# A recurrence in 64 by 64 quarters: products, masks and loads from step 2 on, in a kernel of recurrence and two gated layers on one core

## The chip, the core and the metric

The kernel runs on one core of a Trainium2 chip. The core has TensorE (PE; PEld is its weight load), VectorE (DVE), ScalarE (ACT), GpSimd (POOL) and SyncE (SP), whose instruction stream issues nearly all DMAs here. The metric is the device time of one execution in microseconds (us). Before the change three runs took 878.15, 882.37 and 885.78 us, so the median is 882.37 us.

## What is computed

The reference is a linear recurrence over 768 positions for 4 batches of 8 heads of 48 features, and then two gated layers on its output (3072 rows of 384 features):

```python
for t in range(S):                       # S = 768, state: [4, 8, 48, 48]
    cur = einsum('bhd,bhe->bhde', u * kt, vt)
    y[:, :, t] = einsum('bhd,bhde->bhe', rt, state + cur)
    state = w[:, :, None] * state + einsum('bhd,bhe->bhde', kt, vt)
x = y as [3072, 384]
x = (x @ w_a * (x @ w_b)) @ w_out                    # 384 -> 1536 -> 384
x = ((x @ w1 * (x @ w2)) @ w3) @ w_out2              # 384 -> 1024 -> 384
```

## The kernel before

**The recurrence in chunks.** The 768 positions are cut into six steps of C = 128, and a step has four units, one for each batch; unit `u = 4 * step + batch`, 24 in all. A unit multiplies r and k by tables of powers of w, forms for each head the 128 by 128 scores k·r of positions inside the chunk, masks them to earlier positions, puts the u-weighted value on the diagonal, and adds (scores × v) to (state × r). It then decays the state and adds k × v.

**Heads on the array.** Heads lie in four pairs (`NP = 4`): the even head of a pair at partitions 0 to 47, the odd one at 64 to 111 (`XR`). So the scores' products (`scores_f`, line 343) use 48 rows and all 128 columns, two at a time in the two row halves, each row half with a PSUM bank of its own. `y_mm` multiplies the block-diagonal state by r for a whole pair (line 414, 112 by 112), then all 128 positions of v by the masked scores (line 425, 128 rows by 48 columns, two at a time in the two column halves). `s_mm` (line 497) is 128 rows by 48 columns as well. In steps 0 and 1, where the weights have to be read and converted at the same time, `scores_h` and `scores_d` (lines 358 to 373) already cut a chunk's positions into halves of 64: their products use 48 rows by 64 columns, and four stand in the array at a time.

**Masks and copies.** `a_evac` (line 397, DVE) masks the scores of four heads at a time out of PSUM, `a_diag` (line 403, DVE) writes the diagonal. The output of `y_mm` is split into a rounded high part (`y_evac_h`, ACT) and a low part (`y_evac_l`, DVE); the features of heads 6 and 7 are moved to their places by small DMAs (`y_shuffle`). `s_decay` is ACT, `s_upd` DVE.

**Loads.** A unit loads r and k transposed (`load_rk`, one DMA) and r, k, v in natural order (`load_nat`, one DMA of 576 KB from step 2 on), both on SP's queue, into two buffers each. On the natural copy POOL forms r·u·k (`prep_d`), which DVE sums to the diagonal (line 329), and POOL scales k (`k_nat`).

**The gated layers.** For each step, `block1` goes through twelve slices of 128 hidden features: 18 products of 128 by 128 by 512 (`ab_mm`, line 557) into two of the three banks `ab0` to `ab2`, ACT and DVE form the gated value and its high and low part, and 9 products (`m_mm`, lines 574 to 576) add it to three banks `m0` to `m2`. The second layer (from about 440 us) needs no recurrence.

**What sets the order.** All work is recorded as tasks with an engine, an assumed duration, dependencies, a priority and buffers (`Task`, `Buf`, `Slot`). `plan` (line 95) then walks through an assumed time and writes the instructions of every engine in the order in which they would start; the engines run that order, and wait for each other by semaphores. From step 2 on the recurrence's PSUM tiles come from the two banks `at0` and `at1` alone (`at_c = at_s`), in steps 0 and 1 from these and the `ab` banks.

The functions that the change touches, and what calls them:

Of the kernel before, what the change touches and what calls it, by code (L numbers as in the profile page):

```python
# [7 lines left out]
F32 = mybir.dt.float32  # L8
# [11 lines left out]
NP = H // 2  # L20
# [11 lines left out]
HALF = C // 2  # L32

# [131 lines left out]
def rwkv_moe_kernel(ctx, tc, rkT, nat, wu, wab, wout, w12, w3T, wo2, r_in, k_in, v_in, w_in, u_in, out):  # L165
# [13 lines left out]
    with tc.manual_schedule():  # L179
# [21 lines left out]

        XR = [(0, D), (64, 64 + D)]


# [126 lines left out]
        def k_nat(u):  # L331
            if u < NU - B:
# [3 lines left out]
                eng.tensor_tensor(out=kn_t[u], in0=k, in1=tnat.rearrange("p a x d -> p (a x d)"), op=ALU.mult)  # L336

        def scores_f(ps, r, k):

            for p in range(NP):  # L340
                s = slice(p * C, (p + 1) * C)
                for x, (r0, r1) in enumerate(XR):
                    mm(ps[x][:, p, :], lhsT=k[r0:r1, s], rhs=r[r0:r1, s], start=True, stop=True)  # L343

        def scores(u):
            for x in range(2):
                at_ps[u, x] = at_tile([128, NP, C])
            scores_f([at_ps[u, x] for x in range(2)], flat(rf_t[u]), kf_t.pop(u))
# [45 lines left out]
        def a_evac(u, hf):  # L394
            if hf == 0:
                a_t[u] = att.tile([128, H, C], F32, name="a_sc", bufs=1)
            nc.vector.tensor_tensor(
                out=a_t[u][:, 4 * hf:4 * hf + 4, :], in0=at_ps.pop((u, hf)),
                in1=mask.rearrange("p (o n) -> p o n", o=1).to_broadcast([128, 4, C]), op=ALU.mult)

        def a_diag(u, hf):
            d = d_t[u].rearrange("p (q x) -> p x q", x=2)[:, hf, :]
            nc.vector.copy_predicated(
                out=a_t[u][:, 4 * hf:4 * hf + 4, :],
                mask=ident.bitcast(I32).rearrange("p (o n) -> p o n", o=1).to_broadcast([128, 4, C]),
                data=d.rearrange("p (h o) -> p h o", o=1).to_broadcast([128, 4, C]))

        def y_mm(u):
            c, b = divmod(u, B)
# [6 lines left out]
            if c == 1:  # L416
                for n, e in enumerate((HALF, 128)):
                    for h in range(H):
                        r0, r1 = XR[h % 2]
                        mm(ps[r0:r1, h // 2, n * HALF:(n + 1) * HALF], lhsT=v[0:e, h * D:(h + 1) * D],  # L420
                           rhs=a[0:e, n, h % 2 * 4 + h // 2, :], start=False, stop=True, skip_group_check=True)
            else:
                for h in range(H):
                    r0, r1 = XR[h % 2]
                    mm(ps[r0:r1, h // 2, :], lhsT=v[:, h * D:(h + 1) * D], rhs=a[:, h % 2 * 4 + h // 2, :],  # L425
                       start=False, stop=True, skip_group_check=True)
            rf_t.pop(u)

        def y_0(u):
# [5 lines left out]
            for n, e in enumerate((HALF, 128)):  # L435
                cs = slice(n * HALF, (n + 1) * HALF)
                for k in range(KD):
                    for x in range(2):
                        mm(ps[64 * x:64 * x + 64, k, cs], lhsT=vz[0:e, k, x, :], rhs=a[0:e, n, 4 * x + 3, :],
                           start=(k == 0 and n == 0), stop=False, skip_group_check=True)  # L440
                    for x in range(2):
                        h = 2 * k + x
                        mm(ps[64 * x:64 * x + D, k, cs], lhsT=v_0[0:e, u, h * D:(h + 1) * D], rhs=a[0:e, n, 4 * x + k, :],
# [13 lines left out]
        def y_evac_h(u):  # L457
            c, b = divmod(u, B)
            if b == 0:
                xt[c] = xtp.tile([128, 2, KD, TB], F32R, tag=X_TAG[c], name="xt")  # L460
                y3_t[c] = att.tile([112, 2, TB], F32R, name="y3", bufs=1)
            xh, xl = xt[c][:, 0], xt[c][:, 1]
            ps = at_ps["y", u]
            cs = slice(b * C, (b + 1) * C)
            t = y3_t[c]
# [1127 lines left out]
```

## Time and profile before

| | |
|---|---|
| three runs | 878.15, 882.37, 885.78 us |
| the profiled execution, and its span | 879.93 us, 878.2 us |
| PE busy | 857.5 us, 98% of the span |
| PEld, DVE, ACT, POOL busy | 729.0, 584.5, 396.3, 188.0 us |
| mean granted clock of TensorE | 0.982 |

The profile is of one execution, with times in us from the start of its span. A matmul on 32-bit floats appears as two records, so a group of 8 products of this kind is "x16". A record's length is a latency, and records overlap; what a group of products takes from PE is read from the start of its first record to the start of the next group. The granted clock has two levels here, 1.2 and 2.4 GHz, shown as 0.5 and 1.

### The profile page before, as it was taken

What the parts mean: (1) busy time and instruction counts of PE and PEld (TensorE: products, weight loads), DVE (VectorE), ACT (ScalarE), POOL (GpSimd) and SP (SyncE); (2) the same over time, 40 slices, a digit from 0 to 9 for tenths busy, and PEclk for the clock granted to TensorE, in tenths of its full rate; (3) what the DMA queues carried; (4) which work ended last, traced back from release to release, by engine and by line L of the source; (5) the groups of instructions that cost most, each with busy time, mean ns of one, the idle gap of its engine ahead of it and who ended that gap; (6) DMA issues with size and microseconds to landing.
All of it is one profiled execution on the core that took longest, in us unless ns stands there. A gap on an engine that the chain in (4) does not pass through costs nothing.

```text
span 878.2 us, 14225 instructions
## 1 busy us (share of the span) xinstructions
PE 857.5 (98%) x5307; PEld 729.0 (83%) x5307; DVE 584.5 (67%) x1028; ACT 396.3 (45%) x921; POOL 188.0 (21%) x152
## 2 busy tenths in 40 slices
PE   8889999999999999999999999999999999999996
PEld 7767788887887888888888888888888988898886
DVE  7879989566689768742565558626558845864642
ACT  7644334665675573322256545425327232623222
POOL 0003012035354004210200302211424501511210
PEclk9879899999999999999999999999999999999999
DMA  9454533577799765810164414135545344424202
GB/s 266 163 181 150 185 119 121 182 242 236 235 307 263 258 217 175 242 62 31 55 174 142 135 51 148 53 114 176 175 135 182 112 126 142 157 67 156 90 1 75
DMA packets 59610, 133.97 MB, mean 153 GB/s; under 512 B 6608, under 2 KB 33872, under 8 KB 59536
## 3 DMA queue, kind: packets, MB, share of 16 engines
q1 hardware_dynamic: 59248, 132.61, 47.4%
q8 instruction: 44, 0.72, 0.3%
q10 hardware_dynamic: 288, 0.39, 0.1%
q14 instruction: 30, 0.25, 0.1%
HBM read 107.94 MB, written 23.07 MB: 149 GB/s over the span
## 4 chain that ended last, share of the span: by engine, by line
PE 87%; DVE 7%; DMA 3%; issue 1%; ACT 0%; POOL 0%; SPq 0%; DVEq 0%; POOLq 0%; ACTq 0%
PE ab L557 31%; PE ab L1187 14%; PE m L574 5%; PE m L575 5%; PE m L576 5%; PE at L1187 5%; PE at L1094 4%; PE o L1290 4%; PE o L1292 4%; PE o L1291 4%; DMA raw<-in_wab_dram 2%; PE at L343 2%; PE at L425 1%; PE at L414 1%; DVE cvt L873 1%
## 5 line engine op out<-in xcount | busy, mean ns | idle before, releaser
L662 DVE TENSOR_TENSOR ab<-g,ab 128x512 f32<-128x512 f32 x72 | 50.0, 695 | 70.2 <-PE ab L557 57.7
L1260 DVE TENSOR_TENSOR qx<-qx,ab 128x512 f32<-128x512 f32 x95 | 64.2, 686 | 32.6 <-PE ab L1187 32.1
L574 PE MATMUL m<-gh,woh 128*128 128x512 f32 x216 | 85.2, 395 | 0.0
L575 PE MATMUL m<-gl,woh 128*128 128x512 f32 x216 | 84.3, 390 | 0.0
L576 PE MATMUL m<-gh,wol 128*128 128x512 f32 x216 | 84.2, 390 | 0.0
L664 ACT CAST gh<-ab 128x512 fp32r<-128x512 f32 x72 | 42.1, 585 | 87.0 <-DVE ab L662 84.5
L661 ACT COPY g<-ab 128x512 f32<-128x512 f32 x72 | 42.2, 586 | 72.9 <-PE ab L557 72.9
L1198 POOL TENSOR_TENSOR qx<-qx,qx 128x512 f32<-128x512 f32 x29 | 39.0, 1356 | 124.2 <-DVE qx L1260 117.4
L667 DVE TENSOR_TENSOR gl<-ab,gh 128x512 fp32r<-128x512 f32 x72 | 49.5, 687 | 23.6 <-ACT gh L664 23.4
L1280 ACT CAST gh<-qx 128x512 fp32r<-128x512 f32 x48 | 29.6, 620 | 74.3 <-PE o L1291 48.7
L315 POOL TENSOR_TENSOR rk<-rk,tr 112x512 f32<-112x512 f32 x16 | 22.6, 1414 | 181.7 <-DMA rk<-in_rkT_dram 108.0
L848 ACT ACTIVATE sq<-raw 128x512 bf16<-128x512 f32 x61 | 40.8, 670 | 41.1 <-DMA raw<-in_w_dram 18.3
L1282 DVE TENSOR_TENSOR gl<-qx,gh 128x512 fp32r<-128x512 f32 x48 | 37.4, 785 | 32.4 <-ACT gh L1280 31.1
L1254 ACT ACTIVATE qx<-ab 128x512 f32<-128x512 f32 x56 | 33.1, 599 | 56.9 <-PE ab L1187 55.6
L557 PE MATMUL ab<-xt,wab0h 128*128 128x512 f32 x144 | 48.5, 419 | 2.7 <-DVE gl L667 2.0
L877 DVE SCALAR_TENSOR_TENSOR cvt<-raw,cvt 128x512 int32<-128x512 int32 x61 | 47.6, 780 | 1.5
L574 PEld LDWEIGHTS m<-gh,woh 128*128 128x128 f32 x216 | 40.5, 188 | 9.0 <-issue 0.2
L576 PEld LDWEIGHTS m<-gh,wol 128*128 128x128 f32 x216 | 40.6, 188 | 8.6
L575 PEld LDWEIGHTS m<-gl,woh 128*128 128x128 f32 x216 | 40.5, 188 | 8.0
L557 PE MATMUL ab<-xt,wab2h 128*128 128x512 f32 x144 | 46.9, 408 | 0.0
L557 PE MATMUL ab<-xt,wab1h 128*128 128x512 f32 x144 | 45.7, 398 | 0.0
L873 DVE SCALAR_TENSOR_TENSOR cvt<-raw,cvt 128x512 int32<-128x512 int32 x61 | 43.8, 718 | 1.6
(316 smaller groups left out, 2274.5 us busy)
## 6 DMA issues: line engine op xcount, KB each, us to landing
tg<-t_d SPq DMA_DIRECT2D x45, 640.0 KB, 4.0
raw<-in_wab_dram SPq DMA_DIRECT2D x36, 512.0 KB, 5.0
rk<-in_rkT_dram SPq DMA_DIRECT2D x24, 448.0 KB, 5.3
t_d<-part SPq DMA_DIRECT2D x75, 128.0 KB, 3.8
raw<-in_wout_dram SPq DMA_DIRECT2D x18, 512.0 KB, 4.9
natt<-in_nat_dram SPq DMA_DIRECT2D x16, 576.0 KB, 6.6
raw<-in_w3T_dram SPq DMA_DIRECT2D x16, 512.0 KB, 4.0
raw<-in_w_dram SPq DMA_DIRECT2D x12, 512.0 KB, 4.1
```

The lines of the kernel that those rows point to most:

```text
L557: mm(ps, lhsT=w[i][:, k, cs], rhs=x[:, j, k, :], start=(k + i + j == 0), stop=(k == KD - 1 and i == 1))
L574: mm(m_ps[q][k], lhsT=wh[:, j, cs], rhs=gh, start=first, stop=False)
L575: mm(m_ps[q][k], lhsT=wh[:, j, cs], rhs=gl, start=False, stop=False)
L576: mm(m_ps[q][k], lhsT=wl[:, j, cs], rhs=gh, start=False, stop=last)
L661: ea = use(task("ACT", D_A, lambda x=bg, y=ba: nc.scalar.copy(out=x.ap, in_=y.ap), [a], p0 + 1, [bg]), ba)
L662: mu = use(task("DVE", D_TT, lambda x=bg, y=bb: nc.vector.tensor_tensor(out=y.ap, in0=x.ap, in1=y.ap, op=ALU.mult), [ea, b], p0 + 2), bg, bb)
L664: hi = use(task("ACT", D_A, lambda x=bh, y=bb: nc.scalar.copy(out=x.ap[0], in_=y.ap), [mu], p0 + 2, [bh]), bb)
L667: nc.vector.tensor_tensor(out=x.ap[1], in0=y.ap, in1=x.ap[0], op=ALU.subtract)
L873: nc.vector.scalar_tensor_tensor(out=t["f"], in0=t["w"][:, :, 1], scalar=-0x40000000, in1=t["f"], op0=ALU.bitwise_and, op1=ALU.bitwise_or)
L877: nc.vector.scalar_tensor_tensor(out=t["f"], in0=t["w"][:, :, 0], scalar=29, in1=t["f"], op0=ALU.logical_shift_right, op1=ALU.bitwise_or)
L1187: mm(bank, lhsT=x, rhs=y, start=(start and n == 0), stop=(stop and n == 2), skip_group_check=True)
L1260: e = use(task("DVE", D_TT, lambda bv=bv, b=bank[c], s=s: nc.vector.tensor_tensor(out=bv.ap, in0=bv.ap, in1=b.ap, op=ALU.add if s > 0 else ...
```

## The change

- From step 2 on `scores`, `a_evac` and the branch of `y_mm` for these steps go. `state_scores` forms state × r and the scores in one task: 8 products of state blocks (48 rows, 48 or 64 columns, 128 moving), and 16 of scores (48 rows, 64 columns; 8 with 128 moving, 8 with 64). Heads 0 to 3 and 4 to 7 are two groups `g`, positions of a chunk are two halves `f`: partitions 0 to 63 now hold group 0, partitions 64 to 127 group 1 (`GS`).
- `y_split` adds scores × v (64 rows by 48 columns, 8 products with 128 moving and 8 with 64) and, but for the last step, forms k × v (16 products of 64 rows by 48 columns) into the same two banks.
- `a_mask` (2 DVE instructions of 256), `a_off` (2 ACT copies of 128) and `a_diag` (1 DVE instruction of 512) take the place of 2 + 2 DVE instructions of 512.
- The output comes out of two banks, one for each group: three ACT and three DVE instructions instead of two and two. `s_upd` has four instructions of 96 instead of two of 192.
- `load_nat` from step 2 on is six DMAs (three arrays by two groups) instead of one; u is loaded by four DMAs instead of one; of each slice of the first layer's input weights, the third chunk comes by two DMAs with its partition halves exchanged, because heads 4 and 5 change sides in x. A second table `tnat` is made for the new layout (`tables_s`, 8 products).
- From step 2 on the scores come into two of the three `ab` banks, and state, y and k × v into both `at` banks.
- The plan has other assumed durations and priorities for these tasks: the masks of steps 1 to 5 get an earlier one, step 2 a later one, and the second reading of the weights (for a range test) a later one. So the order of steps 0 and 1 changes in places too.

The diff, cut to its core:

```diff
+        GS = [slice(0, 64), slice(64, 128)]
+        def out_at(h):
+            return 64 * (h % 2 ^ h // 4)
...
             elif u < NU:
                 nat_t[u] = att.tile([128, 3, DM], F32, name="natt")
-                n0 = 1 if u < 2 * B else 0
-                nc.sync.dma_start(out=nat_t[u][:, n0:, :], in_=nat[u, :, n0:, :])
+                if u < 2 * B:
+                    nc.sync.dma_start(out=nat_t[u][:, 1:, :], in_=nat[u, :, 1:, :])
+                    return
+                for n in range(3):
+                    for g in range(2):
+                        nc.sync.dma_start(out=nat_t[u][GS[g], n].rearrange("i (f c) -> i f c", f=2),
+                                          in_=nat[u, :, n, g * HG:(g + 1) * HG].rearrange("(f i) c -> i f c", f=2))
...
+        def state_scores(u):
+            b = u % B
+            t = [at_tile([128, 512]) for _ in range(2)]
+            at_ps["y", u] = [x[:, 0:2 * C].rearrange("p (q t) -> p q t", q=2) for x in t]
+            at_ps["s", u] = [x[:, 384:384 + 2 * D].rearrange("p (q d) -> p q d", q=2) for x in t]
+            for q in range(2):
+                for g, x in ((0, 1), (1, 0), (0, 0), (1, 1)):
+                    p, (r0, r1), c = 2 * g + q, XR[x], 64 * (x ^ g)
+                    e = min(c + 64, 112)
+                    mm(at_ps["y", u][g][c:e, q, :], lhsT=s_t[b][r0:r1, p, c:e], rhs=rf_t[u][r0:r1, p, :], start=(q == 0),
+                       stop=False, skip_group_check=True)
+            for x in range(2):
+                at_ps[u, x] = at_tile([128, 3, 2, HALF])
+            r, k = flat(rf_t[u]), kf_t.pop(u)
+            for q in range(2):
+                for g in range(2):
+                    for x, (r0, r1) in enumerate(XR):
+                        c = (2 * g + q) * C
+                        mm(at_ps[u, x][GS[g], 0:3:2, q, :], lhsT=k[r0:r1, c:c + HALF], rhs=r[r0:r1, c:c + C], start=True,
+                           stop=True)
+                for g in range(2):
+                    for x, (r0, r1) in enumerate(XR):
+                        s = slice((2 * g + q) * C + HALF, (2 * g + q + 1) * C)
+                        mm(at_ps[u, x][GS[g], 1, q, :], lhsT=k[r0:r1, s], rhs=r[r0:r1, s], start=True, stop=True)
...
+        def a_mask(u, x):
+            if x == 0:
+                a_t[u] = att.tile([128, 3, 2, 2, HALF], F32, tag="a_sc", name="a_sc", bufs=1)
+            nc.vector.tensor_tensor(out=a_t[u][:, 0:2, :, x, :].rearrange("p f q n -> p (f q) n"),
+                                    in0=at_ps[u, x][:, 0:2].rearrange("p f q n -> p (f q) n"), in1=bch(mask_h, 4), op=ALU.mult)
+        def a_off(u, x):
+            nc.scalar.copy(out=a_t[u][:, 2, :, x, :], in_=at_ps.pop((u, x))[:, 2])
...
+        def y_split(u):
+            a, v = a_t.pop(u), nat_t[u][:, 2, :].rearrange("p (f c) -> p f c", f=2)
+            four = ((0, 0), (1, 1), (0, 1), (1, 0))
+            for q in range(2):
+                for f in range(2):
+                    for g, x in four:
+                        ps, c = at_ps["y", u][g], 64 * (x ^ g)
+                        v_h = v[GS[g], f, (2 * q + x) * D:(2 * q + x + 1) * D]
+                        if f == 0:
+                            mm(ps[c:c + D, q, :].rearrange("p (f n) -> p f n", f=2), lhsT=v_h, rhs=a[GS[g], 0:3:2, q, x, :],
+                               start=False, stop=True, skip_group_check=True)
+                        else:
+                            mm(ps[c:c + D, q, HALF:], lhsT=v_h, rhs=a[GS[g], 1, q, x, :], start=False, stop=True,
+                               skip_group_check=True)
+            if u < NU - B:
+                kn = kn_t.pop(u).rearrange("p (f c) -> p f c", f=2)
+                for q in range(2):
+                    for f in range(2):
+                        for g, x in four:
+                            hs = slice((2 * q + x) * D, (2 * q + x + 1) * D)
+                            mm(at_ps["s", u][g][XR[x][0]:XR[x][1], q, :], lhsT=kn[GS[g], f, hs], rhs=v[GS[g], f, hs],
+                               start=False, stop=(f == 1), skip_group_check=True)
...
+                by, bt = [Buf(at_s, none) for _ in range(2)], [Buf(banks, none) for _ in range(2)]
+                sc = use(task("PE", 1.5, lambda u=u, bs=by + bt: picked(bs, lambda: state_scores(u)),
+                              [t] + after + s_up.get(u - B, []), pu, by + bt), rk_b[u])
...
+                y = use(task("PE", 1.4 if kn else 1.1, lambda u=u: y_split(u), [ev] + of + kn, pu + 1), al, nat_b[u], ba, *by)
...
+                s_up[u] = [use(task("DVE", 0.85, lambda u=u: s_upd(u), [s_new, sd] + ([] if c == 1 else ev_y), pu + 3), *bs)]
```

Three places show how the instructions now stand. The first is PE in unit 10, the third of step 2 (`at`, `ab`, `m` are the PSUM banks' tiles, `s_164` the state of batch 2, `wab` the first layer's weights). Before, from the scores on (four more rows like the second and third, and six of `wab4h` and `wab4l`, stand at the mark):

```order
L343 MATMUL at<-rk 128x128 x8
L557 MATMUL ab_2136<-xt,wab3h 128x512 x2
L557 MATMUL ab_2136<-xt,wab3l 128x512
...
L414 MATMUL at<-rk,s_164 112x128 x4
L425 MATMUL at<-a_sc,natt 48x128 x8
L497 MATMUL at<-natt,kn 48x48 x8
```

In the changed kernel (at the first mark more rows of the same kinds; at the second, the seven others of the nine `m` products):

```order
L405 MATMUL at<-rk,s_164 48x128 x2
L405 MATMUL at<-rk,s_164 64x128 x2
...
L414 MATMUL ab<-rk 64x2x64 x4
L419 MATMUL ab<-rk 64x64 x4
L640 MATMUL m_2297<-gh_2239,woh_1252 128x512
L641 MATMUL m_2297<-gl_2240,woh_1252 128x512
...
L623 MATMUL ab_2325<-xt,wab4h 128x512 x2
L623 MATMUL ab_2325<-xt,wab4l 128x512
L447 MATMUL at<-a_sc,natt 48x128 x4
L450 MATMUL at<-a_sc,natt 48x64 x4
L458 MATMUL at<-natt,kn 48x48 x16
```

State × r has moved ahead of the masks, and between the scores and what needs the masks there now stand 12 products of 512 instead of 18.

The second is PE in unit 13, the second of step 3, in the changed kernel:

```order
L419 MATMUL ab<-rk 64x64 x4
L623 MATMUL ab_2784<-xt,wab0h 128x512 x2
L623 MATMUL ab_2784<-xt,wab0l 128x512
L623 MATMUL ab_2863<-xt,wab0h 128x512 x2
L623 MATMUL ab_2863<-xt,wab0l 128x512
L447 MATMUL at<-a_sc,natt 48x128 x4
```

and DVE at the same place, where two sums of the first layer's output (`m_2297`, `m_2298`) and the diagonal of the next unit stand ahead of the masks:

```order
L700 TENSOR_TENSOR g_2837<-m_2297,m_part 128x512
L340 TENSOR_REDUCE dg<-pr 128x8
L700 TENSOR_TENSOR g_2848<-m_2298,m_part 128x512
L427 TENSOR_TENSOR a_sc<-ab,mask_h 128x4x64 x2
L434 COPY_PREDICATED a_sc<-ident_h,dg 128x512
```

Here only 6 products stand between scores and masks' use, and the second three of them (`ab_2863`) need an `ab` bank that the scores of this unit hold.

The third is SP's queue in step 2, before:

```order
L212 DMA rk<-in_rkT_dram 112x1024
L222 DMA natt<-in_nat_dram 128x1152
L839 DMA raw<-in_wout_dram 128x512
L839 DMA raw<-in_wab_dram 128x512
L839 DMA raw<-in_w_dram 128x512
```

and in the changed kernel:

```order
L218 DMA rk<-in_rkT_dram 112x1024
L232 DMA natt<-in_nat_dram 64x2x192 x6
L925 DMA raw<-in_wab_dram 128x512
L1025 DMA w_d<-cvt 128x2x128 x2
L925 DMA raw<-in_w_dram 128x512
```

The natural-order load takes six places of the queue, and what follows it stands five issues later.

## Rows read from the trace of the kernel before

**Rows 1.** The page's 40 slices: PE's busy tenths and its granted clock.
```profile
PE   8889999999999999999999999999999999999996
PEclk9879899999999999999999999999999999999999
```

**Rows 2.** Busy time by stretch (PE, PEld, DVE, ACT, POOL; granted clock; DMA share; GB/s).
```profile
44.00:54.00 10.00, 7.67 (x17) 5.63 (x18) 7.46 (x15) 4.46 (x12) 0.00 (x0) 0.53 0.61 205
92.00:176.00 84.00, 84.00 (x410) 69.48 (x409) 66.87 (x108) 38.26 (x81) 8.84 (x7) 1.00 0.48 148
```

**Rows 3.** PE's timeline in unit 10 (start, us, line, out<-in, rows*columns, shape, count).
```profile
188.23 1.16 PE L343 MATMUL at<-rk 48*128 48x128 f32 x16
189.32 0.73 PE L557 MATMUL ab<-xt,wab3h 128*128 128x512 f32 x2
...
193.54 1.04 PE L414 MATMUL at<-rk,s 112*112 112x128 f32 x8
...
195.42 0.53 PE L497 MATMUL at<-natt,kn 128*48 128x48 f32 x16
195.88 0.50 PE L557 MATMUL ab<-xt,wab4h 128*128 128x512 f32 x1
```

**Rows 4.** The same in the last unit, 23.
```profile
434.71 1.04 PE L414 MATMUL at<-rk,s 112*112 112x128 f32 x8
...
436.68 0.50 PE L557 MATMUL ab<-xt,wab1h 128*128 128x512 f32 x1
```

**Rows 5.** PE's timeline, 16 products of step 1 (`scores_d`), four in the array at a time.
```profile
68.99 0.27 PE L372 MATMUL ab<-rk,alt 48*64 48x64 f32 x1
...
69.16 0.22 PE L372 MATMUL ab<-rk,alt 48*64 48x64 f32 x1
69.17 0.22 PE L372 MATMUL at<-rk,alt 48*64 48x64 f32 x1
69.17 0.22 PE L372 MATMUL ab<-rk,alt 48*64 48x64 f32 x1
69.18 0.22 PE L372 MATMUL at<-rk,alt 48*64 48x64 f32 x1
...
69.45 0.22 PE L372 MATMUL ab<-rk,alt 48*64 48x64 f32 x1
...
69.62 0.50 PE L574 MATMUL m<-gh,woh 128*128 128x512 f32 x1
```

**Rows 6.** The same, products of 128 moving in `scores_h`.
```profile
66.06 0.28 PE L358 MATMUL at<-alt 48*64 48x128 f32 x2
...
66.28 0.28 PE L358 MATMUL at<-alt 48*64 48x128 f32 x2
```

**Rows 7.** Groups by line (count; busy us, mean ns; idle before it, releaser).
```profile
L382 DVE TENSOR_TENSOR a_sc<-at,mask_h 128x256 f32<-128x256 f32 x4 | 1.6, 416 | 0.4 <-PE at L362 0.4
L403 DVE COPY_PREDICATED a_sc<-ident,dg 128x512 f32<-128x512 int32 x32 | 31.6, 1041 | 0.0
L504 ACT ACTIVATE s<-s,wC 112x112 f32<-112x112 f32 x64 | 19.7, 389 | 0.0
```

**Rows 8.** Line 222, the natural-order load: issue (ns, min/median/max), and time to landing.
```profile
L222 SPq DMA_DIRECT2D natt<-in_nat_dram x20: 328/370/429, 13.0 to 416.3; - x20
DMA to landing us min/median/max: 3.0/6.6/9.9
```

**Rows 9.** DVE's timeline in unit 12: its diagonal's sum, and the first use of it.
```profile
209.49 0.55 DVE L329 TENSOR_REDUCE dg<-pr 128x8 f32<-128x384 f32 x1 [1.37 <-POOL pr L326]
...
215.66 2.06 DVE L403 COPY_PREDICATED a_sc<-ident,dg 128x512 f32<-128x512 int32 x2
```

**Rows 10.** PE's waits (whom, us in total, times, longest).
```profile
PE ab L557 <- DVE gl L667: 2.0, 1, 2.0
PE at L425 <- DVE a_sc L403: 0.7, 1, 0.7
PE at L343 <- DVE s L514: 0.5, 1, 0.5
```

More of the change, by code (lines that the diff above doesn't have):

```diff
@@ L335, in k_nat @@
                 eng = nc.vector if u < 2 * B else nc.gpsimd
[L336 to L348, printed above, removed]
+                eng.tensor_tensor(out=kn_t[u], in0=k, in1=tnat[0].rearrange("p a x d -> p (a x d)"), op=ALU.mult)
         def scores_h(u):
@@ L771, in rwkv_moe_kernel @@
             ln = task("SP", 0.4, lambda u=u: load_nat(u), [], pu - 100, [nat_b[u]], size=0.39 if c == 1 else 0.58)
-            at_c = at_s + banks if c == 1 else at_s
-            bt = [Buf(at_c, none) for _ in range(2)]
+            at_c = at_s + banks
+            ba = Buf(a_s, none)
+            kn = []
+            if u == 2 * B:
+                bt = Buf(at_c, none)
+                tn = use(task("PE", 0.9, lambda bt=bt: picked([bt], tables_s), s_kn, due(82), [bt]), tmp_b)
+                tn = use(task("ACT", 0.6, tables_n, [tn], due(82)), bt)
+            if c < NC - 1:
+                bk = Buf(kn_s, none)
+                eng, d = ("DVE", 0.55) if c == 1 else ("POOL", 1.15)
+                kn = s_kn = [use(task(eng, d, lambda u=u: k_nat(u), [ln, tn] + s_kn, pu, [bk]), nat_b[u])]
             if c == 1:
-                al, bd = alt_b[b], [Buf(at_c, none) for _ in range(2)]
+                bt, bd = ([Buf(at_c, none) for _ in range(2)] for _ in range(2))
+                al = alt_b[b]
                 pu_ = use(task("ACT", 1.3, lambda u=u: prep_0(u, 2), [lr], pu - 9), rk_b[u], al)
@@ new lines, in rwkv_moe_kernel @@
+                by, bt = [Buf(at_s, none) for _ in range(2)], [Buf(banks, none) for _ in range(2)]
+                sc = use(task("PE", 1.5, lambda u=u, bs=by + bt: picked(bs, lambda: state_scores(u)),
+                              [t] + after + s_up.get(u - B, []), pu, by + bt), rk_b[u])
+                of, ev = [], []
+                for x in range(2):
+                    ev = [use(task("DVE", 0.42, lambda u=u, x=x: a_mask(u, x), [sc] + ev, pu - 300, [] if x else [ba]), bt[x], ba)]
+                    of.append(use(task("ACT", 0.28, lambda u=u, x=x: a_off(u, x), ev, pu - 300), bt[x], ba))
@@ L835, in rwkv_moe_kernel, with raw @@
         done, loads = {}, []
[L837 removed]
+        def raw(t, br, src, swap=False):
             t["r"] = stg.tile([128, 512], I64, tag=br.ap, name="raw")
[L839 removed]
+            if swap:
+                for g in range(2):
+                    nc.sync.dma_start(out=t["r"][GS[g]], in_=src[GS[1 - g]])
+            else:
+                nc.sync.dma_start(out=t["r"], in_=src)
         def check(n, t, br, ld, prio):
@@ L856, in rwkv_moe_kernel, with convert @@
         again = []
-        def convert(n, src, dst, prio, parts=None, into=(), after=(), first=False):
+        def convert(n, src, dst, prio, parts=None, into=(), after=(), first=False, swap=False):
             br, bc = Buf(s_all if first else raw_s, none), Buf(cvt_all if first else cvt_s, none)
@@ L909, in rwkv_moe_kernel @@
                 again.append((n_chunk, src))
-                ends.append(convert(n_chunk, src, None, due(us + 2.8 * k), parts, into, head, True))
+                ends.append(convert(n_chunk, src, None, due(us + 2.8 * k), parts, into, head, True,
+                                    kind == "ab" and k == 2))
                 head = highs[-1:]
```

184 lines of the change are left out of this document (91 added, 93 removed).

## The prediction

> **What bounds the kernel now.** I read the page's 40 slices first: PE is busy nine tenths or more in all but the first slices and the last, and its granted clock leaves the upper level only in the first five [rows 1]. The stretches say the same with numbers: from 92 to 176 us PE is busy for all 84.00 us at clock 1.00 while DVE has 66.87, and before that there are stretches such as 44 to 54 us, where PE is busy 7.67 of 10 us at 0.53, with a wait of 2.0 us for DVE in it [rows 2, 10]. So from step 2 on, where the change is made, time is what PE's products take. A shorter DVE, ACT or POOL gives nothing there unless PE waits for it, and from step 2 on PE's one wait for the masks is 0.7 us [rows 10]. I therefore count PE's groups from the start of one to the start of the next.
>
> **What goes.** In unit 10 the scores take 188.23 to 189.32, 1.09 us; state × r, scores × v and k × v take 193.54 to 195.88, 2.34 us, of which k × v is 0.46 [rows 3]. Together 3.43 us, and twelve units have this shape. The four units of the last step have no k × v: 434.71 to 436.68 is 1.97 us, with the scores 3.06 [rows 4]. In all 12 × 3.43 + 4 × 3.06 = 53.4 us of PE's time.
>
> **What comes.** The nearest rows are step 1's products in four quarters. Four records with 64 moving start at 69.16 to 69.18, and five such sets take 69.16 to 69.45, 0.058 us a set; sixteen products, 32 records, take 68.99 to 69.62, 0.63 us, which is 8 × 0.058 = 0.46 and a fixed 0.17 for getting in and out [rows 5]. With 128 moving a set takes 0.11 us (two from 66.06 to 66.28) [rows 6]. A set is four records, and a product has two records, so:
>
> - `state_scores`: 8 state products are 4 sets of 128; the scores are 4 sets of 128 and 4 of 64. 8 × 0.11 + 4 × 0.058 + 0.17 = 1.28 us.
> - `y_split`: 4 sets of 128 and 4 of 64, 0.67 us, and for k × v 8 sets with 48 moving. One such set is at least (0.46 − 0.17) / 8 = 0.036 us, if it is like the pairs of [rows 3], and at most the 0.058 of 64 columns; I take 48/64 of the latter, 0.044, since those rows too are quarters. 0.67 + 0.35 + 0.17 = 1.19 us, and 0.84 us in the last step.
> - `tables_s`, once: 16 records of 112 moving, two at a time. Eight sets scaled from 0.11 give 0.8 us, one at a time they take 1.6; I take 0.9, near the first, since all other rows with two column halves go in pairs.
>
> That is 16 × 1.28 + 12 × 1.19 + 4 × 0.84 + 0.9 = 39.1 us, 14.3 less. Bounds: without the fixed 0.17 anywhere and with 0.036 for the narrow sets the new groups take 32.8 us (20.6 less); with the fixed part paid twice in a group, since each now has two or three kinds of product, 0.058 and 1.6, they take 46.4 us (7.0 less).
>
> The Trainium skill (TensorE: Matmul & The Clock Gate, "Wait — 56ns, not 53.3ns?") says that starts of matmuls are never closer than about 25 ns however few columns move. By it the 64 records of a `y_split` would take 1.60 us before the fixed part, and the sum of all groups would grow by some 9 us. The trace disagrees: 32 records in 0.63 us are 20 ns each with everything, and four start within 0.02 us [rows 5]; I go by the trace.
>
> **Waits between the two groups.** `y_split` needs masks and diagonal of the scores. Before, 18 products of 512 lay between, now 12 (6 in unit 13, 18 in unit 16). The 18 take 189.32 to 193.54, 4.22 us [rows 3], so 12 give 2.8 us. The new chain on DVE is two masks of 256 at 0.416 and one diagonal at 1.04 in the mean, 1.9 us [rows 7]; the old one had twice the width in both. So the cover is enough by 0.9 us, and what hides the masks is the gated layer's own products; without them each unit would cost 1.9 us, 30 us in all. ACT's two copies `a_off` can stand behind `s_decay`, 4 × 0.389 = 1.6 us [rows 7], and still end within the 2.8. Unit 13 is the exception: two sums of 512 (at most twice a mask of 256, 0.83 each) and a `dg` of 0.55 [rows 9] go ahead of its masks. They begin when PE begins `state_scores`, so masks end after 2.2 + 0.8 and the copies some 0.4 later, 3.4 us; PE has done its 1.28 and three products (0.7) by 2.0 and cannot start the next three, whose bank the scores hold. Between nothing, if the sums are done earlier, and 1.4 us; I take 1.2. Against it the old wait of 0.7 for the masks goes [rows 10]. Net 0.5 us lost.
>
> **Other parts.** One more instruction each on ACT and DVE for the output, two more for the state, two copies on ACT: all beside PE, and DVE is given back more by the halved masks. The banks are tighter: a unit's `state_scores` now waits for the state's update of the unit before, since both `at` banks are held from one to the other. At least 15 products of 512, 3.5 us, stand between two units of a step in the new order, and the update is made beside these; PE waited for such an update once, 0.5 us [rows 10]. I count nothing; rival 4 prices it. SP: 16 units × 5 more issues at 0.37 us, 1.9 us a unit [rows 8]. In unit 12 the diagonal is summed by 210.04 and first used at 215.66 [rows 9], 5.6 us of slack, which covers that. In the first 92 us the order shifts in several places; nothing there is made of other products, so I take 0, with one low-clock stretch like that of [rows 2] more or less, 10 × 0.47 = 4.7 us, as bounds.
>
> **Sum.** −14.3 + 0.5 = −13.8 us. The profiled execution took 879.93 us (its span is 878.2), so the changed one should take 866.1. It lies 2.4 below the median of the three runs, 882.37; on that footing I predict **868.6 us**.
>
> **Rivals.**
>
> 1. *The state products go two at a time.* In all rows with four quarters each row half writes a bank of its own (`ab` and `at` alternate in [rows 5]). In `state_scores` the two row halves of one group write one bank, in different partition halves; no row shows that. If PE lets only one row half at a time into a bank, 4 sets become 8, 0.44 us more in 16 units, 7.0 us: 875.6 us. The Trainium skill (TensorEngine Tiling (Array Packing), "Gotcha 1: PSUM Pressure") states: "Different row tiles cannot access same PSUM bank simultaneously". By that rule this rival holds; it says that software must see to it, not that the engine waits, and nothing here shows either. For it speaks that rule alone, against it that column halves share a bank freely in [rows 3]. Chance 0.13.
> 2. *The first 92 us get one more stretch at the lower clock*, since the gaps there lie elsewhere in the new order and a wait of 2.0 us came with one [rows 2, 10]. 4.7 us: 873.3 us. As likely the other way, which my range's lower end takes in. Chance 0.09.
> 3. *Slower than before: the natural-order loads come too late.* One DMA lands after 6.6 us, at most 9.9 [rows 8]. Six pieces, if they are served one after another, take up to six times the least landing, 3.0, so 18 us. From 5.6 us of added lateness on, the diagonal is late and `y_split` waits; the two buffers then pass it on. Each us beyond costs 14 us over the units of steps 2 to 5 that are not loaded ahead. Two beyond it: 868.6 + 28 = 896.6 us. Against it: even 9.9 and 1.9 us of issues are 5.2 us later than 6.6, still inside. Chance 0.05.
> 4. *PE's gain is as counted but other waits eat half of it* (the update of the state ahead of the next `state_scores`, in every unit what it cost once, 0.5 us [rows 10]): 16 × 0.5 = 8.0 us, 876.6 us. For it: both banks are held now. Against: the same two banks served before, and it came once in 16 units. Chance 0.08.
>
> **Numbers.** My forecast has 0.65, its own range by the bounds 861 to 876. The range for 8 in 10 runs from 860 (20.6 less and part of an early stretch saved) to 877 (rivals 1, 2 and 4 with a little each way). About 1%, 8.8 us, is what a measurement of this kernel can tell from no change. Below 873.5 lie nearly all of the forecast (0.61), half of rival 2 and a third of rivals 1 and 4, since a median of three runs can lie 2 or 3 us off: faster 0.73. Same 0.22, slower 0.05, the whole of rival 3.
>
> **What would show it.** Right: `state_scores` start to next start near 1.28 us, `y_split` near 1.19 and 0.84; records of state × r in sets of four 0.11 us apart; PE's waits for masks only in unit 13. Rival 1: state records in pairs, `state_scores` near 1.7. Rival 3: POOL's first product waits for `natt`, and `y_split` for DVE in most units. Wrong altogether: the groups as short as said and the time not, which would put the loss into the first 92 us.

## The result, and the profile after

The changed kernel takes **871.7 us** (median of 12 runs, 869.2 to 875.3), the kernel before 881.4 in the runs beside it: ratio 0.9899, 95% interval 0.9873 to 0.9925, 9.7 us less. Forecast were 868.6 us and 13.8 less. The profiled execution took 875.25 us (span 873.5), the longest of the 12; it lies 4.7 below the profiled 879.93 of before, so the two traces show less of a gain than the medians.

The page's slices, which answer to [rows 1]: PE is nearly as full as before, and its granted clock is below nine tenths in the first two slices and the last. Slices 11 and 16, in which PE is a tenth less busy than its neighbours, hold the two longest waits.

```profile
PE   8899999999899998999999999999999999999996
PEclk8699999999999999999999999999999999999998
```

Busy time by stretch (columns as in [rows 2]), first of the changed kernel, then of the kernel before:

```profile
0.00:92.00 92.00, 82.68 (x1186) 68.59 (x1187) 78.95 (x163) 52.12 (x145) 11.60 (x17) 0.89 0.68 194
92.00:176.00 84.00, 83.98 (x511) 68.84 (x511) 62.45 (x111) 41.63 (x91) 8.68 (x7) 1.00 0.55 162
176.00:440.00 264.00, 254.13 (x2419) 204.28 (x2419) 163.95 (x398) 118.83 (x352) 76.24 (x62) 0.99 0.58 167
```
```profile
0.00:92.00 92.00, 80.80 (x1156) 67.44 (x1157) 77.42 (x151) 50.24 (x134) 12.16 (x17) 0.85 0.60 192
176.00:440.00 264.00, 262.12 (x1680) 215.70 (x1679) 178.52 (x377) 128.77 (x360) 75.59 (x62) 1.00 0.61 193
```

The third row is the finding: from 176 to 440 us, where nearly all of the changed products run, PE now stands idle for 264 − 254.13 = 9.9 us, before it was 1.9. The products themselves came out as counted. PE's timeline, unit 9's `y_split`, unit 21's `state_scores`, and the last step's `y_split`, answering to [rows 3, 4]:

```profile
178.42 0.44 PE L447 MATMUL at<-a_sc,natt 64*48 64x128 f32 x8
...
179.12 0.54 PE L458 MATMUL at<-natt,kn 64*48 64x48 f32 x32
179.59 0.73 PE L623 MATMUL ab<-xt,wab3h 128*128 128x512 f32 x2
...
406.34 0.67 PE L405 MATMUL at<-rk,s 48*48 48x128 f32 x16
406.82 0.41 PE L414 MATMUL ab<-rk 48*64 48x128 f32 x8
...
407.61 0.50 PE L640 MATMUL m<-gh,woh 128*128 128x512 f32 x1
...
410.56 0.44 PE L447 MATMUL at<-a_sc,natt 64*48 64x128 f32 x8
...
411.36 0.50 PE L623 MATMUL ab<-xt,wab0h 128*128 128x512 f32 x1
```

Start to next start: `state_scores` 407.61 − 406.34 = 1.27 us, `y_split` 1.17, in the last step 0.80. `tables_s` is 16 records in 1.42 us, about 1.35 to the next start:

```profile
80.49 1.42 PE L604 MATMUL at<-ident,tmp 112*64 112x112 f32 x16
```

In sum 16 × 1.27 + 12 × 1.17 + 4 × 0.80 + 1.35 = 38.9 us (forecast 39.1). The 53.4 of before gone, that is 14.5 less. PE's waits (whom, us in total, times, longest), which answer to [rows 10]:

```profile
PE ab L623 <- ACT a_sc L431: 4.5, 3, 2.9
PE at L447 <- ACT a_sc L431: 2.9, 2, 2.2
...
PE at L447 <- DVE a_sc L434: 0.3, 1, 0.3
...
PE at L405 <- DVE s L570: 0.2, 1, 0.2
```

L431 is the copy `a_off`, the end of the chain from the scores to `y_split`: 7.4 us in five waits. After the two longest, 2.9 us at 230 and 2.25 at 333, the granted clock stood at its lower level, 1.2 GHz, for 3.4 us each (the column ahead of the last two):

```profile
234.20:237.60 3.40, 3.40 (x63) 2.92 (x54) 0.90 (x3) 1.51 (x5) 1.00 (x1) 0.50 0.61 176
336.60:340.00 3.40, 3.40 (x35) 2.73 (x24) 3.28 (x9) 1.82 (x10) 1.00 (x1) 0.50 0.81 260
```

That costs half of each, 3.4 us together. The first 92 us give as much back: their mean granted clock is 0.89 where it was 0.85, and over the whole span it is 0.982 in both profiled executions, so the clock explains none of the difference between them.

The account of the two executions is then short. PE is busy for 846.7 us by the page, where it was busy for 857.5, 10.8 less. It is idle for 26.8 us of the span instead of 20.7, 6.1 more: 8.0 more between 176 and 440 us, 1.9 less before 92 us (9.3 against 11.2). Together that is the 4.7 measured.

So PE's busy time fell by 10.8 us and not by the 14.5 of the groups. Reading a group from its start to the next start leaves out what it does to the product ahead of it. That product's record is 0.39 us long, and among its own kind it takes 0.23 us to the next start. Ahead of `y_split` (178.42) it takes 0.32; ahead of the 112 by 112 products of before (193.54) it took 0.23. First the changed kernel, unit 9, then the kernel before, unit 10:

```profile
178.10 0.39 PE L623 MATMUL ab<-xt,wab3l 128*128 128x512 f32 x1
```
```profile
193.31 0.39 PE L557 MATMUL ab<-xt,wab4l 128*128 128x512 f32 x1
```

Twelve units have no wait just ahead of `y_split`, so this is 12 × 0.09 = 1.1 us. A product that is followed by a wait also counts as busy for its whole 0.39 us; the rest of the 3.7 us isn't traced.

**Why the copies are late.** The masks and copies themselves are as short as [rows 7] had it; the diagonal and other work of DVE are not always (ns, min/median/max, of single lines):

```profile
L427 DVE TENSOR_TENSOR a_sc<-ab,mask_h x32: 407/416/425, 144.2 to 428.9; 128x256 f32<-128x256 f32 x32
L431 ACT COPY a_sc<-ab x32: 242/265/283, 144.6 to 429.3; 128x128 f32<-128x128 f32 x32
L434 DVE COPY_PREDICATED a_sc<-ident_h,dg x16: 727/760/2362, 145.0 to 429.3; 128x512 f32<-128x512 int32 x16
L1096 DVE TENSOR_TENSOR wt<-wt,wa x6: 283/292/2501, 275.5 to 356.6; 128x128 f32<-128x128 f32 x6
```

Unit 18 in the timeline, all engines (L326 to L337 are POOL's four products for a later unit, L1096 and L1076 sums and splits of the second layer's weights, L427 the masks):

```profile
328.95 1.28 POOL L326 TENSOR_TENSOR rk<-rk,tr 112x512 f32<-112x512 f32 x1 [3.66 <-DMA rk<-in_rkT_dram]
329.12 2.50 DVE L1096 TENSOR_TENSOR wt<-wt,wa 128x128 f32<-128x128 f32 x1
...
330.18 1.29 POOL L330 TENSOR_TENSOR rk<-rk,tk 112x512 f32<-112x512 f32 x1
...
331.42 1.07 POOL L335 TENSOR_TENSOR pr<-natt,u_bc 128x384 f32<-128x384 f32 x1
331.54 1.10 DVE L1076 TENSOR_TENSOR part<-wa,part 128x128 fp32r<-128x128 f32 x1
...
332.57 1.01 POOL L337 TENSOR_TENSOR pr<-pr,natt 128x384 f32<-128x384 f32 x1
332.67 1.05 DVE L1096 TENSOR_TENSOR wa<-wt,wa 128x128 f32<-128x128 f32 x1
...
333.97 0.75 DVE L427 TENSOR_TENSOR a_sc<-ab,mask_h 128x256 f32<-128x256 f32 x2
...
335.58 0.45 PE L447 MATMUL at<-a_sc,natt 64*48 64x128 f32 x5 [2.25 <-ACT a_sc L431]
```

PE had finished the scores at 330.3 and the 12 covering products at 333.3. DVE's three small instructions ahead of the masks take 2.50, 1.10 and 1.05 us here; the median of their lines is 0.29. Each ends about 0.15 us after a POOL instruction does. The masks, which read one operand from PSUM, did not stretch: all 32 took 407 to 425 ns. The Trainium skill (SBUF — State Buffer, "Who interferes with whom") says that a DVE instruction with two inputs in SBUF contends with a GpSimd instruction that reads SBUF, for a pair of ports that is an exclusive lock. The trace agrees, with 2.50 us beside 0.29. The diagonal's predicated copy stretches too, up to 2.36 us.

The longest wait, 2.9 us in unit 13, has other causes:

```profile
229.67 0.55 DVE L340 TENSOR_REDUCE dg<-pr 128x8 f32<-128x384 f32 x1 [2.01 <-POOL pr L337]
229.97 0.66 ACT L934 ACTIVATE sq<-raw 128x512 bf16<-128x512 f32 x1 [4.80 <-DMA raw<-in_w_dram]
...
232.59 0.40 ACT L431 COPY a_sc<-ab 128x128 f32<-128x128 f32 x2
```

DVE stood 2.01 us for POOL's product before it could sum the next diagonal, which lies ahead of the masks; these ended at 231.49. ACT had waited 4.80 us for a load of weights, and its work on that load and the four instructions of `s_decay` then held the copies back for another 1.1 us.

The second suspect is the load. Line 232 against [rows 8]:

```profile
L232 SPq DMA_DIRECT2D natt<-in_nat_dram x96: 595/605/1410, 74.3 to 414.8; - x96
DMA to landing us min/median/max: 2.5/3.9/6.1
```

A piece takes SP 0.605 us, not 0.370, so a unit's six take 3.6. Before, PE held the chain of what ended last from 176 to 203 us. Now this queue and loads stand in it from 182 us on, with ACT, DVE and POOL between; three pieces of it:

```profile
182.76 0.93 SPq L232
...
204.25 4.04 DMA raw<-in_w_dram
...
212.24 6.96 DMA raw<-in_w_dram
```

The weights' loads themselves are not slower: between 176 and 362 us the medians of their kinds lie 4.0 to 5.1 us after the issue, before 4.0 to 5.3.

### The profile page after: what moved, and what is told of

It reads as the page before. It is cut to its first block, busy times and chain, and to the rows that moved or that the text cites. A ratio compares the mean times of both kernels' runs of the same rounds, so it can differ in the third digit from the quotient of the medians.

```text
span 873.5 us, 16133 instructions
## 1 busy us (share of the span) xinstructions
PE 846.7 (97%) x6155; PEld 713.7 (82%) x6155; DVE 567.5 (65%) x1060; ACT 407.6 (47%) x979; POOL 189.1 (22%) x152
## 4 chain that ended last, share of the span: by engine, by line
PE 79%; DVE 10%; DMA 5%; issue 2%; ACT 1%; SPq 1%; POOL 0%; DVEq 0%; POOLq 0%; ACTq 0%
PE ab L623 26%; PE ab L1274 14%; PE at L1274 5%; PE m L641 4%; PE m L640 4%; PE m L642 4%; PE at L1181 4%; PE o L1377 4%; PE o L1379 4%; PE o L1378 4%; DMA natt<-in_nat_dram 2%; DVE cvt L963 1%; DVE cvt L959 1%; DMA raw<-in_w_dram 1%; DMA rk<-in_rkT_dram 1%
## 5 line engine op out<-in xcount | busy, mean ns | idle before, releaser
L326 POOL TENSOR_TENSOR rk<-rk,tr 112x512 f32<-112x512 f32 x16 | 21.3, 1330 | 179.3 <-DMA rk<-in_rkT_dram 175.5
L934 ACT ACTIVATE sq<-raw 128x512 bf16<-128x512 f32 x61 | 41.0, 672 | 25.5 <-DMA raw<-in_w_dram 13.8
L623 PE MATMUL ab<-xt,wab0h 128*128 128x512 f32 x144 | 46.6, 406 | 2.9 <-ACT a_sc L431 2.9
L963 DVE SCALAR_TENSOR_TENSOR cvt<-raw,cvt 128x512 int32<-128x512 int32 x61 | 48.3, 792 | 1.3
L959 DVE SCALAR_TENSOR_TENSOR cvt<-raw,cvt 128x512 int32<-128x512 int32 x61 | 46.7, 765 | 1.5
```

Of the source, the lines that this page charges most:

```text
L623: mm(ps, lhsT=w[i][:, k, cs], rhs=x[:, j, k, :], start=(k + i + j == 0), stop=(k == KD - 1 and i == 1))
L959: nc.vector.scalar_tensor_tensor(out=t["f"], in0=t["w"][:, :, 1], scalar=-0x40000000, in1=t["f"], op0=ALU.bitwise_and, op1=ALU.bitwise_or)
L963: nc.vector.scalar_tensor_tensor(out=t["f"], in0=t["w"][:, :, 0], scalar=29, in1=t["f"], op0=ALU.logical_shift_right, op1=ALU.bitwise_or)
```

## The experiments

Each row below is PE's busy time in the 264 us from 176 to 440 us; what is missing to 264 are its waits. Times are medians; in brackets stand the ratio to the kernel before, in runs beside it, and its 95% interval. The kernel before took 878.5 to 881.4 us in these groups of runs.

**e1: POOL's products cut, changed kernel**

```diff
-            eng.tensor_tensor(out=r, in0=r, in1=flat(tr), op=ALU.mult)
+            n = 512 if u < 2 * B else 8
+            eng.tensor_tensor(out=r[:, 0:n], in0=r[:, 0:n], in1=flat(tr)[:, 0:n], op=ALU.mult)
...
-                nc.vector.tensor_reduce(out=d_t[u], in_=pr_t.pop(u), op=ALU.add, axis=AX.X)
+                nc.vector.tensor_reduce(out=d_t[u], in_=nat_t[u][:, 1, :].rearrange("p (h d) -> p h d", h=H), op=ALU.add,
+                                        axis=AX.X)
```

> Theory P (POOL holds DVE up): the gain in PE's products is all there, and what is missing went into waits of steps 2 to 5 for the masks and the copies behind them, because a DVE instruction with two inputs in SBUF stands still while POOL runs, and the masks stand behind such instructions in DVE's queue. Theory O (order): the masks are late because the written-out order puts too many DVE instructions ahead of them, whatever POOL does. Theory A (ACT): the copies are late because ACT's queue is full ahead of them. This kernel is the changed one in the same order, with POOL's four products of each unit of steps 2 to 5 cut to 8 columns, so their results are not the reference's; the sums of the diagonal read the loaded k instead. P expects L1096's instructions at 0.28 us throughout, masks within 0.5 us of the end of the scores in all units but 13, PE's idle time between 176 and 440 us down from 9.9 to 2 to 4 us, and 864 us (862 to 867) where the changed kernel took 871.7. O expects the same waits and 870 to 873. A expects the same waits on the copies, with masks early, and 870 to 872.

```profile
176.00:440.00 264.00, 260.93 (x2495) 210.67 (x2488) 155.89 (x411) 124.88 (x364) 22.08 (x62) 0.99 0.62 176
```

864.1 us (ratio 0.9823, 0.9793 to 0.9853), 7.6 below the changed kernel, with 3.1 us of waits; the masks were over 0.5 us late in units 10 and 15 alone. P's time and its waits hold; as the whole cause, O and A are out. The sums of the second layer's weights are short again but for one of 0.99 us.

**e2: the same cut in the kernel before**

> The kernel before with the same cut of POOL's four products in steps 2 to 5 (results of these not the reference's). There PE waited only 1.9 us between 176 and 440 us, so P expects little, 879 to 881 where 881.4 was, and a distance of 15 to 18 us to the changed kernel with the same cut: the whole of what PE's products save (15.0 us in the two traces) and what waits and low-clock stretches gave. O and A expect the distance to stay where it is now, 9.7 us, within 2.

```profile
176.00:440.00 264.00, 264.00 (x1688) 217.96 (x1687) 161.15 (x380) 130.96 (x362) 24.76 (x62) 1.00 0.63 194
```

871.6 us (0.9907, 0.9882 to 0.9933): 8.0 less, where P expected 0 to 2. The distance to e1 is 7.5, which is not what P expected. POOL had cost the kernel before as much. In the profiles PE's waits fall by 1.9 us in this stretch and by 2.4 before 92 us, and rise by 1.7 between; where the rest of the 8.0 lies isn't shown. Shown is that POOL stood in the length of the diagonal, which I had taken for its price. The diagonal's line in the kernel before, and then in e2 (ns, min/median/max):

```profile
L403 DVE COPY_PREDICATED a_sc<-ident,dg x32: 712/736/1839, 113.4 to 432.4; 128x512 f32<-128x512 int32 x32
```
```profile
L409 DVE COPY_PREDICATED a_sc<-ident,dg x32: 716/731/741, 110.6 to 425.8; 128x512 f32<-128x512 int32 x32
```

So P alone can't say why the changed kernel keeps only 7.5 us. By the pages PE is busy 11.0 us less in e1 than in e2 (842.4 and 853.4), and the 3.1 us of waits that e1 has here, and e2 has not, account for most of the difference between 11.0 and 7.5.

**e3 and e4: a planner that knows of it**, on the changed kernel and on the one before

```diff
+        if t.lock:
+            at = max(at, held["DVE" if e == "POOL" else "POOL"])
         picks = []
...
+        if t.lock:
+            held[t.eng] = t.end + 0.02
```

(`lock` is set for POOL's tasks and for DVE's with two inputs in SBUF.)

> The changed kernel, with one thing more that the planner knows: a DVE instruction with two inputs in SBUF (the conversions, the sums and splits of the second layer's weights, the diagonal) can't start while a POOL instruction runs, and the other way round; nothing is computed otherwise. It puts the masks ahead of such instructions where POOL is at work. P expects masks within 0.5 us of the end of the scores in nearly all units, PE's idle time between 176 and 440 us down to 2 to 5 us, and 866 us (864 to 869). O expects some of it too, since masks move ahead in the order, but with waits left where DVE's queue is long: 868 to 871. A expects 870 to 873.

> The kernel before with the same addition to the planner. PE waited 1.9 us between 176 and 440 us there, and 2.0 and 0.7 us for DVE in the first 92. P expects no gain from steps 2 to 5: 879 to 883, where 881.4 was; a change beyond 2 us would have to come from the order in the first 92 us, by the low-clock stretches there.

e3, then e4:

```profile
176.00:440.00 264.00, 254.49 (x2427) 204.75 (x2427) 161.57 (x398) 121.93 (x362) 71.97 (x62) 0.99 0.61 174
```
```profile
176.00:440.00 264.00, 264.00 (x1688) 217.95 (x1687) 175.80 (x376) 131.56 (x367) 74.75 (x62) 1.00 0.62 195
```

e3 took 870.1 us (0.9885, 0.9857 to 0.9914), e4 873.8 (0.9930, 0.9904 to 0.9956). Both are misses for P; e3 lies in O's range. The kernel before loses its last wait and gains 6, where nothing was expected. As its expectation allowed, much of that stands in the first 92 us of its profile: 1.2 us less of waits and a clock of 0.89 instead of 0.85. So e4 doesn't price the rule. The changed kernel keeps 9.5 us of waits, in other places. Its masks start within 0.1 us of the end of the scores in eleven units and 0.6 to 2.9 us late in five, and PE waits for the gated layer's own evictions instead:

```profile
PE ab L629 <- DVE gl L743: 5.4, 3, 2.4
```

The longest of these stood behind a DVE instruction that waited 7.3 us for a load of weights. That led to theory D.

**e5 and e6: one DMA in place of six**, e6 with the planner of e3 too

```diff
-                for n in range(3):
-                    for g in range(2):
-                        nc.sync.dma_start(out=nat_t[u][GS[g], n].rearrange("i (f c) -> i f c", f=2),
-                                          in_=nat[u, :, n, g * HG:(g + 1) * HG].rearrange("(f i) c -> i f c", f=2))
+                nc.sync.dma_start(out=nat_t[u], in_=nat[u])
```

> Theory D (loads): the six pieces in which r, k and v of a unit are loaded keep SP's queue busy, so the loads of weights behind them land later than the order counts on; ACT's first and DVE's first instruction on such a load then stand in line ahead of what PE needs. Against it theory P alone: POOL holds DVE up, and the pieces cost nothing, as predicted. This kernel is the changed one in the same order, with the natural-order input laid out by the host as the tile holds it, so that one DMA of 576 KB takes the place of six of 96 KB in each unit of steps 2 to 5. D expects PE's idle time between 176 and 440 us down from 9.9 to 4 to 7 us and 866 to 869, where the changed kernel took 871.7. P alone expects 870.5 to 873.

> The changed kernel with both: the one DMA of e5, and the planner of e3 that knows that POOL and a DVE instruction with two inputs in SBUF exclude each other. The version before with that planner had no wait left from step 2 on and took 873.8. If waits of these two kinds (P and D) are all that is missing from the gain in PE's products, this takes 873.8 less 13 to 15, 859 to 862, with PE's idle time between 176 and 440 us under 3 us. If neither is the cause, it stays with e3, 869 to 871.

e5, then e6:

```profile
176.00:440.00 264.00, 256.98 (x2489) 206.68 (x2488) 170.61 (x405) 122.55 (x360) 75.94 (x62) 1.00 0.57 174
```
```profile
176.00:440.00 264.00, 259.72 (x2410) 210.15 (x2409) 168.45 (x412) 127.43 (x369) 72.17 (x61) 1.00 0.59 181
```

e5: 868.9 us (0.9871, 0.9838 to 0.9904), just within D's time, with its 7.0 us of waits at the upper end. Its interval overlaps the changed kernel's (0.9873 to 0.9925), so by itself it doesn't show D. e6: **863.7 us** (0.9818, 0.9790 to 0.9847), the fastest of the kernels that leave nothing out, 10.1 below e4; expected were 13 to 15, and the 4.3 us of waits left account for most of the rest. Against e3, the same planner with six pieces, it is 6.4 us faster, and the intervals don't overlap. One place in the traces agrees with D: from the issue of a unit's r and k, at 219.3 us in both, to that of the next load of weights the changed kernel takes 6.8 us and e5 2.8. e5 and e6 also read longer rows than the six pieces do; they don't separate that from the time of the issues.

**e7: the load part alone**, on the kernel before

```diff
+                for n in range(3):
+                    for g in range(2):
+                        cs = slice(g * DM // 2, (g + 1) * DM // 2)
+                        nc.sync.dma_start(out=nat_t[u][:, n, cs], in_=nat[u, :, n, cs])
```

> The load part of the change alone: the kernel before, with its one load of r, k and v of a unit of steps 2 to 5 cut into six, three tensors by two halves of the columns, rows of 768 bytes as in the changed kernel, into the layout it had. D expects waits in the stretch from 176 to 362 us and 883 to 886, where the kernel before took 879.7 in the last call. P alone expects no difference, 879 to 881.

```profile
L227 SPq DMA_DIRECT2D natt<-in_nat_dram x96: 327/430/1814, 73.8 to 416.3; - x96
```

881.5 us, ratio 1.0014 (0.9984 to 1.0045): no difference shown, and D's 883 to 886 not reached; its waits in the stretch are 3.1 us, against 1.9. Its pieces are cheaper to issue than those of the change, 0.430 us against 0.605, and the order before has more cover (18 products); so it doesn't measure the price of the change's load, and D rests on e6 against e3 and e8 against e1.

**e8: both causes taken away** (e1 and e5 together)

> The changed kernel with POOL's four products of a unit cut to 8 columns (e1; these results are not the reference's) and the one DMA of e5. e1 took 864.1 with 3.1 us of waits left between 176 and 440 us, behind loads of weights. D expects these gone: 860 to 862, and a distance of 10 to 12 us to e2, the kernel before with the same cut. P alone expects 864, as e1.

```profile
176.00:440.00 264.00, 262.90 (x2426) 213.19 (x2425) 158.88 (x414) 127.44 (x367) 22.14 (x61) 1.00 0.59 177
```

857.6 us (0.9746, 0.9716 to 0.9776), below D's range; 1.1 us of waits are left. Against e1 it is 6.5 us faster, and the intervals don't overlap. The distance to e2 is 14.1 us, more than D's 10 to 12. That it is close to the 14.5 of the groups is in part chance: in the profiles the first 92 us ran at a clock of 0.93 in e8 and 0.89 in e2, worth 3.7 us (0.04 × 92, an estimate), and e8 waited 3.1 us less before 176 us.

**e9: the changed kernel again**

> The changed kernel once more, on the chip of this call, for a second profile. Its first profiled execution was the longest of its runs (875.3 where the median was 871.7) and had 9.9 us of waits of PE between 176 and 440 us. If these come from the order and not from that execution, as P and D both say, the second profile has 7 to 10 us there too, at the units 10, 13, 18 and 20 above all, and the median lies within 870 to 873.

```profile
176.00:440.00 264.00, 252.87 (x2415) 203.43 (x2414) 165.00 (x395) 118.22 (x350) 72.47 (x62) 0.99 0.57 165
```

872.1 us (0.9920, 0.9895 to 0.9946), that is 6.4 below the 878.5 of before in these runs, where the first measurement had 9.7. It has 11.1 us of waits, more than the 7 to 10 expected, the longest 2.5 and 2.4 us in units 10 and 18. The waits belong to the order and not to one execution; their sizes vary: unit 13 has 1.1 us here, with its masks on time and the copies still behind `s_decay`.

**e10: the planner's numbers nearer to the traces**

```diff
-DMA_0, DMA_MB = 2.0, 3.6
+DMA_0, DMA_MB = 3.0, 3.6
...
-                sc = use(task("PE", 1.5, lambda u=u, bs=by + bt: picked(bs, lambda: state_scores(u)),
+                sc = use(task("PE", 1.3, lambda u=u, bs=by + bt: picked(bs, lambda: state_scores(u)),
```

> The kernel of e6 (863.7) with the planner's numbers nearer to the traces: the groups state_scores and y_split at 1.3 and 1.2 us (0.85 in the last step) in place of 1.5 and 1.4 (1.1), and 1 us more from the end of a transfer's service to its landing, 3.0 in place of 2.0, since the loads of weights landed 4.7 to 5.4 us after their issue. The instructions of ACT and DVE that wait for a load should then stand later in their queues. If what e6 still waits for (4.3 us between 176 and 440 us, behind such instructions) is D's kind, this leaves 1 to 3 us of it and takes 860 to 863. If the order moves at random with the numbers, 862 to 867.

```profile
PE at L374 <- DVE s L573: 3.5, 1, 3.5
...
PE ab L1281 <- ACT qx L1348: 2.3, 1, 2.3
```

873.1 us (0.9937, 0.9916 to 0.9957), a miss by 10 for D and by 6 for an order that moves at random. The waits from 176 to 440 us fell to 2.1 us, as hoped; but the whole order moved. A wait of 3.5 us stands at 70 us now, the first 92 us ran at a mean clock of 0.83 (e6: 0.93), and some 5 us of waits appeared past 590 us, where there were none.

**e11: POOL whole, the sum free of it**

```diff
-                nc.vector.tensor_reduce(out=d_t[u], in_=pr_t.pop(u), op=ALU.add, axis=AX.X)
+                pr_t.pop(u)
+                nc.vector.tensor_reduce(out=d_t[u], in_=nat_t[u][:, 1, :].rearrange("p (h d) -> p h d", h=H), op=ALU.add,
+                                        axis=AX.X)
```

> e1's cut of POOL's products took away two things at once: POOL and DVE at the same memory, and DVE's wait for POOL's product ahead of the diagonal's sum (four such waits, 9.6 us in all, in the changed kernel's trace, one of them ahead of unit 13's masks). This kernel is the changed one in the same order with POOL's four products whole, but the sum reads the loaded k and so waits for nothing of POOL's (its diagonal is not the reference's). If the memory is what counts (P), the masks of units 10, 18 and 20 stay late, L1096's longest instructions stay above 1 us, PE waits 7 to 10 us between 176 and 440 us, and the time is 868 to 872. If it is the wait for the product, 4 us or less of waits are left and it takes 863 to 866, as e1.

```profile
176.00:440.00 264.00, 254.82 (x2435) 204.81 (x2435) 168.35 (x404) 120.46 (x355) 76.18 (x62) 1.00 0.60 172
```

870.7 us (0.9898, 0.9866 to 0.9929), 9.2 us of waits, and the sums of the second layer's weights up to 2.24 us long. So it was not DVE's wait for POOL's product that e1 took away; what helped was that the two engines no longer met at SBUF. (That POOL's buffers come free sooner in e1 is not separated from this.) The masks of units 10 and 20 were late as expected, those of unit 18 on time: which unit is hit depends on how DVE and POOL happen to meet.

## Why the prediction was right, and where it was not

- **What goes and what comes** was right as it was counted, from start to start: 14.3 forecast, 14.5 in the rows. The quarter rows of step 1 [rows 5, 6] priced products of other shapes to 0.04 us a group. `tables_s` was too low, 0.9 for 1.35. But PE's busy time fell by 10.8 only; the sum had no term for the slower product ahead of `y_split`, 1.1 us.
- **Rival 1** is out: 16 state records take 0.48 us (406.34 to 406.82), 0.12 for four; two at a time they would take 0.88. Two row halves wrote one bank, in different partition halves, without waiting. The Trainium skill (TensorEngine Tiling (Array Packing), "Gotcha 1: PSUM Pressure") states that different row tiles cannot access the same bank simultaneously; that did not show here, with 0.12 us for four records.
- **Waits between the two groups** is the step that failed: "the cover is enough by 0.9 us" was right for a DVE that is free when the scores end (units 8, 9, 16, 17, 19 and 21 to 23 lose nothing). Its 0.5 us net were 7.0: 7.7 for copies and diagonal, less the old 0.7. I priced the chain, not the queue in front of it, on DVE and on ACT. Unit 13, the one exception I named, lost 2.9 us and not 1.2: DVE had waited for POOL's product and ACT for a load, and `s_decay` was still ahead of the copies.
- **SP** at nothing was the second: issues of 0.605 us, not 0.370, 3.3 more a unit, not 1.9. The slack I compared them with was that of the load itself, and it held: PE waited for the diagonal just 0.3 us, so rival 3 stayed away. What came late were loads of weights issued behind the six pieces, and ACT and DVE instructions behind those. The medians put this at 3 us in e5, which isn't clear of the noise, and at 6.4 and 6.5 us once POOL's part is planned for or taken away.
- **Rival 4** (other waits eat half, 8.0 us) named the size of the added waits, 8.0 us in the profile, with the wrong cause: the state's update cost PE 0.2 us.
- **The first 92 us** gave 1.9 us of waits back in these two profiles, and by the clock of 0.89 for 0.85 another 3.7 (0.04 × 92, an estimate): 5.6, a little over the 4.7 allowed as a bound, where I had taken 0. The two low-clock stretches after 176 us took 3.4 of it back.

That the time came within 3.1 us of the forecast is in part luck. The gain was 9.7 us, and 6.4 in e9, where 13.8 was forecast: 70 and 46% of it. The range held the time because it had room for waits like these (rivals 2 and 4), not because I had seen them coming, and a gain in the first 92 us that I had put at nothing offset part of them.

The medians differ by 9.7 us where the two profiled executions differ by 4.7. Most of the 5.0 us between is the profiled execution of the changed kernel: its mean granted clock was 0.982, that of its 12 runs 0.981 to 0.992 with a mean of 0.9865. The difference is worth some 3.9 us (0.0045 × 872, an estimate), and it lies 3.6 above the median. The other 1.5 us is that the profiled execution of before lies below its own median.

## What to carry to other kernels

When a change removes cover, price the engine's queue at that place, not only the chain: list what stands ahead of the instruction that PE needs, and how long it can take at its worst row, not in its mean. A mean far above the median of the same form (1.04 against 0.74 for the diagonal) was a wait in disguise here. When groups are read from start to start, read the product ahead of the group too. And read the issue time of a DMA from one of its own shape, then ask whose loads stand behind it in the queue.

## What the runs showed of the hardware that was not expected

- DVE instructions with both operands in SBUF, the predicated copy among them, were held where they met POOL's: 0.29 us became 2.50, 0.74 became 1.84 and 2.36. With POOL's products cut, the 32 diagonals of the kernel before took 716 to 741 ns.
- An issue of a 96 KB piece with a split row pattern took SP 0.605 us, of a plain piece of the same size 0.430, of the whole 576 KB 0.370.
- In the first profile PE's waits of 2.9 and 2.2 us in an otherwise full stretch were each followed by 3.4 us at the lower clock. In e9 one of 1.5 us was too, one of 2.4 us had it from its last 0.3 us on, and one of 2.5 us had none.
- Two row halves of the array wrote one PSUM bank, in different partition halves, without a wait: 16 records of 128 columns in 0.48 us.
